# First chunk's values on SyncE's queue with a cast on chip, and a new rank for every step, in a gated linear attention followed by a mixture of experts

## The chip, the cores and the metric

The kernel runs on one core of one Trainium2 chip. The metric is device time in microseconds (us) of one execution. Five engines work side by side: TensorE (PE, matrix multiplication; PEld is its weight load), VectorE (DVE), ScalarE (ACT), GpSimd (POOL) and SyncE (SP, which here only issues transfers). Transfers (DMA) are issued by SP and by POOL, each with a queue of its own; the transfers that POOL issues can convert a type on the way.

## The reference

```
# attention: B, H, S, D = 4, 8, 768, 48; one state of D x D for each b, h
f = 1 / (1 + exp(-f_logit))
for t in range(S):
    state = f[t][:, None] * state + outer(k[t], v[t])
    y[t] = q[t] @ state
x = y, with the heads of one position side by side      # (3072, 384)
# experts: E = 4, 384 -> 1024 -> 384
p = domain_probs / (sum(domain_probs) + 1e-9)
out = sum over e of  p[:, e] * (relu(x @ w1[e]) @ w2[e])
```

## The kernel before, in words

The sequence is cut into C = 6 chunks of T = 128 positions. Within a chunk attention is done with matrices: the logarithms of the gates are summed along the chunk (`cs`, and `cq` for the queries of chunk 0), exponentials of the sums (`exps`, `expq`) scale q and k (`q`, `k`), both are transposed on PE (`tpq`, `tpk`), the scores `at` are evicted under a triangular mask (`ev_at0`, `ev_at1`; two of them in chunk 0 by ACT with a `mask` step on POOL after it), `y` multiplies the scores with the values v in bf16 (tile `vb`), `kv` and `ev_kv` and `sf` carry the state on. In chunk 0 `y` is evicted, transposed on PE (`xt`) and evicted as x (`ev_xt`). Then follow the experts: `h` is x @ w1 for one expert and 128 (or 4 x 128) columns of the hidden layer, `relu` its eviction, `o` one half of h @ w2 for 128 positions, `ev_o` its weighted sum. Chunk 0 and half of chunk 1 are done so; the other chunks use seven products in place of eight for the second layer (`hs`, `relu_s`, sums `s1` to `s4`, products `p`, L521 to L607).

The order of the work is not that of the source. Every step is declared with `Plan.add` (L64): a name, the engines that may do it with a planned duration for each, what it depends on, which buffers it takes and frees, and a priority. `Plan.run` (L92) then goes through planned time and, for each engine that is free, takes the first step in order of priority whose inputs are ready and whose buffers are free. The list that results is written out once, so each engine has a fixed order on the chip; the chip's own semaphores decide when each step starts. In the kernel before the priority is computed from the step's place in the loops, and a list `MOVES` (L15) shifts some of them. `DMA` is one more engine of the plan; its order is that of SP's queue.

The loads of chunk 0 are the part that the change touches. For each batch b of four, f, k and q (192 KB each) are loaded by SP as fp32 (L290, L292, order at L1035). The values v are loaded by POOL straight into `vb` (L284): a casting transfer, fp32 in memory and 96 KB of bf16 on chip. The weights are loaded by POOL as well, cast to bf16 (L303), in eleven pieces w0 to w10: w0 and w1 are the first layer of expert 0 in two halves, w2 and w3 that of expert 1, w4 and w5 the second layer of expert 0, w6 and later whole layers; w10 is the second layer of expert 3. POOL's own order of transfers is `SEQ` (L1036): v0 v1 v2 w0 v3 w1, then the other weights. `GATE` (L1039) makes the issue of v0 wait until k1 has landed, and that of v1 until k2 has. In later chunks v is loaded by SP as fp32 into the tile `v`, and a step `v` casts it (`cast_v`, L392). Further waits: f1.0 (chunk 1) is issued when w6 has landed, f1.1 when w8 has (L297, L299), w10 when k1.0 has (L307). While PE has nothing to do ahead of the first `h`, it runs matmuls on a constant (L1022) as padding.

Of the kernel before, what the change touches and what calls it, by code (L numbers as in the profile page):

```python
# [14 lines left out]
MOVES = (  # L15
# [21 lines left out]
)  # L37


class Op:  # L40


    def __init__(self, name, costs, emit, prio, deps=(), takes=(), frees=(), lag=0.0):
# [3 lines left out]
        if name.split(" ")[-1].startswith("0.") and {"ACT", "DVE"} & set(costs):  # L47
            self.lag += 0.1
# [5 lines left out]
class Plan:  # L54


    LATENCY = 0.2
# [6 lines left out]
    def add(self, *args, **kw):  # L64
        op = Op(*args, **kw)
# [71 lines left out]
def kernel(  # L137
# [97 lines left out]
    ins = {}  # L235
# [835 lines left out]
```

## Time and profile before

| | us |
|---|---|
| median of 3 runs | 287.46 (287.0 to 287.76) |
| span of the profiled execution, first to last instruction | 285.7 |
| first transfer issued by SP (f0) | 0.80 |
| first expert matmul on PE (L489) | 18.18 |
| first matmul with w10 (L504) | 58.63 |
| last eviction on DVE (L607) starts | 282.41 |

The span is that of one profiled execution, from its first to its last instruction; the time of a run contains what lies around the span as well. In a row of the time line the first two numbers are start and duration, then come engine, line and operation, what it writes and reads, and, in brackets, how long the engine was idle just before and what it waited for. In a row of a group (line, engine, operation, count) stand busy time and mean duration in ns, then the idle time ahead of the group and its releasers. A row for a DMA has its size on chip and the time from issue to landing. A matmul's duration is modelled and covers its way through the array, so rows of PE overlap; what one costs is read from one start to the next.

### The profile page before, as it was taken

What the parts mean: (1) busy time and instruction counts of PE and PEld (TensorE: products, weight loads), DVE (VectorE), ACT (ScalarE), POOL (GpSimd) and SP (SyncE); (2) the same over time, 40 slices, a digit from 0 to 9 for tenths busy, and PEclk for the clock granted to TensorE, in tenths of its full rate; (3) what the DMA queues carried; (4) which work ended last, traced back from release to release, by engine and by line L of the source; (5) the groups of instructions that cost most, each with busy time, mean ns of one, the idle gap of its engine ahead of it and who ended that gap; (6) DMA issues with size and microseconds to landing.
All of it is one profiled execution on the core that took longest, in us unless ns stands there. A gap on an engine that the chain in (4) does not pass through costs nothing.

```text
span 285.7 us, 7476 instructions
## 1 busy us (share of the span) xinstructions
PE 277.4 (97%) x3016; PEld 236.7 (83%) x3020; DVE 196.1 (69%) x402; ACT 180.6 (63%) x336; POOL 114.1 (40%) x186
## 2 busy tenths in 40 slices
PE   6889999999999999999999999999999999999995
PEld 4667555657877999999999998999899998999994
DVE  5794144697779896875888848886888730874374
ACT  6768756568657963586668766658638348836710
POOL 5999101528663760866036756343750000000000
PEclk9999999999999999999999999999999999999999
DMA  6999999999977999999879999989675210050003
GB/s 157 214 199 207 208 192 205 178 202 178 183 142 151 160 197 155 210 184 185 178 150 189 164 224 210 144 191 158 74 164 107 57 55 2 19 122 31 2 0 110
DMA packets 153687, 41.85 MB, mean 146 GB/s; under 512 B 144029, under 2 KB 152861, under 8 KB 153653
## 3 DMA queue, kind: packets, MB, share of 16 engines
q1 hardware_dynamic: 142404, 34.66, 65.0%
q0 software_dynamic: 11248, 6.72, 16.3%
q8 instruction: 23, 0.38, 0.6%
q14 instruction: 12, 0.09, 0.1%
HBM read 31.51 MB, written 4.72 MB: 127 GB/s over the span
## 4 chain that ended last, share of the span: by engine, by line
PE 78%; DMA 14%; POOL 5%; SPq 1%; issue 0%; DVE 0%; POOLq 0%
PE ps_m L521 33%; PE ps_m L580 29%; DMA w_sb<-in_moe_w_dram 10%; PE ps_m L504 6%; PE ps_m L489 4%; DMA k<-in_k_dram 4%; POOL w_sb L303 2%; PE ps_m L428 2%; PE ps_m L455 1%; POOL vb L284 1%; PE ps_m L451 1%; PE ps_m L338 1%; PE ps_m L461 1%; POOL AT L432 1%; SPq L290 1%
## 5 line engine op out<-in xcount | busy, mean ns | idle before, releaser
L521 PE MATMUL ps_m<-x,w_sb 128*128 128x256 bf16 x864 | 104.8, 273 | 0.0
L529 ACT ACTIVATE h<-ps_m 128x512 bf16<-128x512 f32 x111 | 66.2, 598 | 46.1 <-PE ps_m L521 38.8
L521 PEld LDWEIGHTS <-w_sb 128*128 128x128 bf16 x864 | 82.9, 98 | 9.4
L580 PEld LDWEIGHTS <-S 128*128 128x128 bf16 x576 | 48.7, 98 | 0.9
L607 DVE TENSOR_TENSOR o<-ps_m,o 128x192 f32<-128x192 f32 x91 | 31.3, 354 | 22.0 <-PE ps_m L580 21.0
L580 PEld LDWEIGHTS <-h 128*128 128x128 bf16 x432 | 36.2, 98 | 0.6
L504 PE MATMUL ps_m<-w_sb,h 128*128 128x384 bf16 x192 | 35.3, 326 | 0.4 <-DMA w_sb<-in_moe_w_dram 0.4
L489 PE MATMUL ps_m<-x,w_sb 128*128 128x128 bf16 (+2 forms) x260 | 34.5, 281 | 0.6 <-DMA w_sb<-in_moe_w_dram 0.4
L411 ACT ACTIVATE yb<-ps_m,pn 128x384 bf16<-128x384 f32 x54 | 28.1, 584 | 7.7 <-PE ps_m L455 6.4
L476 POOL TENSOR_TENSOR Sf<-Sf,egs 48x192 f32<-48x192 f32 x40 | 21.0, 526 | 27.1 <-DVE Sf L468 17.4
L444 DVE TENSOR_TENSOR AT<-ps_m,mask 128x512 bf16<-128x512 f32 x40 | 25.2, 683 | 8.6 <-PE ps_m L428 8.5
L500 ACT ACTIVATE h<-ps_m 128x512 bf16<-128x512 f32 (+1 forms) x42 | 22.5, 536 | 12.8 <-PE ps_m L489 11.8
L489 PEld LDWEIGHTS <-w_sb 128*128 128x128 bf16 x264 | 21.7, 98 | 9.5 <-DMA w_sb<-in_moe_w_dram 0.6
L544 DVE TENSOR_TENSOR S<-h 128x1024 bf16<-128x1024 bf16 x36 | 25.2, 713 | 6.1 <-ACT h L529 5.5
L580 PE MATMUL ps_m<-ts_sb,S 128*128 128x192 bf16 x288 | 29.2, 246 | 0.0
L580 PE MATMUL ps_m<-w_sb,S 128*128 128x192 bf16 x288 | 28.7, 246 | 0.0
L504 PEld LDWEIGHTS <-h 128*128 128x128 bf16 x192 | 18.3, 98 | 12.5 <-DMA w_sb<-in_moe_w_dram 0.9
L388 POOL TENSOR_TENSOR qk<-q,e 128x384 bf16<-128x384 f32 x19 | 22.7, 1205 | 14.5 <-ACT e L371 9.7
L580 PE MATMUL ps_m<-w_sb,h 128*128 128x192 bf16 x288 | 28.0, 246 | 0.0
L527 DVE TENSOR_SCALAR h<-ps_m 128x512 bf16<-128x512 f32 x33 | 22.4, 691 | 8.1 <-PE ps_m L521 7.5
L371 ACT ACTIVATE e<-ps_m 128x384 f32<-128x384 f32 x40 | 23.4, 704 | 5.8 <-PE ps_m L338 5.4
L388 POOL TENSOR_TENSOR qk<-k,e 128x384 bf16<-128x384 f32 x20 | 20.2, 1016 | 16.7 <-PE ps_m L580 7.4
(87 smaller groups left out, 317.5 us busy)
## 6 DMA issues: line engine op xcount, KB each, us to landing
out_dram<-o SPq DMA_DIRECT2D x23, 192.0 KB, 2.3
w_sb<-in_moe_w_dram POOLq DMA_DIRECT2D x5, 768.0 KB, 16.3
k<-in_k_dram SPq DMA_DIRECT2D x10, 384.0 KB, 5.6
q<-in_q_dram SPq DMA_DIRECT2D x10, 384.0 KB, 5.2
v<-in_v_dram SPq DMA_DIRECT2D x10, 384.0 KB, 5.4
f<-in_f_logit_dram SPq DMA_DIRECT2D x9, 384.0 KB, 4.6
w_sb<-in_moe_w_dram POOLq DMA_DIRECT2D x6, 384.0 KB, 8.6
f<-in_f_logit_dram SPq DMA_DIRECT2D x6, 192.0 KB, 3.7
```

What stands on the lines that cost most here:

```text
L371: nc.scalar.activation(out=o, in_=i, func=AF.Exp, scale=1.0 if j else -1.0)
L388: return engines[eng].tensor_tensor(out=tl("qk", c, b)[:, j, :, 0:D].rearrange("t (i r) d -> t i r d", r=2), in0=tl("qk"[j], c, b // 2)[:, ...
L411: nc.scalar.activation(out=ys, in_=y, func=AF.Copy, scale=pe)
L444: nc.vector.tensor_tensor(out=tl("AT", c, b)[:, r].rearrange("s i t -> s (i t)"), in0=tl("A", c, b, r).rearrange("s i t -> s (i t)"), in1= ...
L489: nc.tensor.matmul(out=hp(c, e, fc, n0, n1, nf)[:, f], lhsT=w1_sb[:, e, kk, (fc + f) * 128:(fc + f + 1) * 128], rhs=tl("xT", c)[:, kk, n0: ...
L500: nc.scalar.activation(out=dst, in_=src, func=AF.Relu)
L504: nc.tensor.matmul(out=tl("op", c, e, nt)[:, 0:Din], lhsT=tl("h", c, e, half_of(c, nt * T))[:, fc, nt * T:(nt + 1) * T], rhs=w2_sb[:, e, f ...
L521: nc.tensor.matmul(out=out_[:, f], lhsT=w1_sb[:, e, kk, (fc + f) * 128:(fc + f + 1) * 128], rhs=tl("xs", c, hf, p)[:, el, kk, :], start=(k ...
L529: nc.scalar.activation(out=dst, in_=tl("hp", c, hf, p, el, fc), func=AF.Relu)
L544: return nc.vector.tensor_tensor(out=o, in0=in0, in1=in1, op=op)
L580: nc.tensor.matmul(out=out_, lhsT=lhs[:, f, :], rhs=rhs[:, f, :], start=(first and el == 0 and f == 0), stop=(el == 1 and f == KH - 1), sk ...
L607: nc.vector.tensor_tensor(out=o, in0=src, in1=o, op=ALU.add)
```

## The change

1. The loads v0 to v3 of chunk 0 go to SP's queue, as fp32 into the tile `v`, in the declared order f0 k0 q0 f1 k1 q1 v0 f2 k2 q2 v1 f3 k3 q3 v2 v3. `SEQ` is gone; POOL's queue holds the weights alone at the start.
2. Four cast steps `v 0.b` are added, on POOL, ACT or DVE.
3. `GATE` now makes the issue of w0 wait until v1 has landed; the two old gates are gone.
4. `MOVES` is replaced by `RANKS`: one number for each of the 1483 steps, in the order in which they are declared, which takes the place of the computed priority; a letter behind it pins the step to ACT (A), DVE (D) or POOL (P).
5. Planned durations are changed, and the planned latency between engines goes from 0.2 to 0.12 us. They act on the order alone.

Read against the steps as they are declared, the ranks give SP's queue the order f0 f1 q0 q1 f2 k1 k0 f3 k2 k3 q2 v1 q3 v0 v2 (probabilities) v3. Some other ranks of the start: expq 0.2 41, gate2 0.3 45, ev_at1 0.1 48 (ACT), q 0.2 50P, v 0.1 56A, mask1 0.1 59 (POOL), issue of w0 63, y 0.1 65, v 0.0 66A, v 0.2 71P, y 0.0 73, xt 0.1 77, issue of w1 79, v 0.3 85P, at 0.3 89, xt 0.0 93, first h 95, y 0.2 104, y 0.3 108. Around w10: cs 1.2 278, o 0.2.1.0 281, o 0.3.2.0 (the first use of w10) 284, o 0.1.3.1 294. A rank is a priority, not yet a place: a step with a higher number goes first where that with the lower one isn't ready in the plan.

```
+RANKS = (
+    "0 8 2 1 6 3 40 4 16 25 29 13 20 35 46 53 63 72 79 88 90 101 107 119 117 132 129 145 137 156 177 153 178 159 193 166 230 "
...
-    LATENCY = 0.2
+    LATENCY = 0.12
...
-        self.moves = dict(m.split("=") for m in MOVES.split(";") if m)
+        self.ranks = RANKS.split()
...
-        by, _, engine = self.moves.get(op.name, "0").partition("@")
-        op.prio += float(by)
-        if engine:
+        rank = self.ranks[len(self.ops)]
+        op.prio = int(rank.rstrip("ADP"))
+        if rank[-1] in "ADP":
+            engine = {"A": "ACT", "D": "DVE", "P": "POOL"}[rank[-1]]
             op.costs = {engine: op.costs[engine]}
...
     def load(c, nm, b, n):
-        if (c, nm) == (0, "v"):
-            ins[c, nm, b] = nc.gpsimd.dma_start(out=tl("vb", c, b), in_=srcs[nm][c, :, b * H:(b + n) * H, :])
-            if f"v{b}" in GATE:
-                after(ins[c, nm, b], ins[GATE[f"v{b}"]])
-            return
...
-        op = P.add(f"ld {nm}{c}.{b}", {"DMA": cost or (1.05 if c else 0.8 if nm in PAIRED else 1.1) * n}, lambda e: load(c, nm, b, n), prio,
-                   deps=deps, takes=[(nm, c, b // 2)], lag=2.0)
+        op = P.add(f"ld {nm}{c}.{b}", {"DMA": cost or (0.85 if c else 0.66 if nm in PAIRED else 0.85) * n}, lambda e: load(c, nm, b, n), prio,
+                   deps=deps, takes=[(nm, c, b // 2)], lag=2.0 if c else 2.5)
...
-        if x[0] == "v":
-            issued.append(P.add(f"v issue {i}", {"POOL": 0.8}, lambda _, i=i: load(0, "v", i, 1), -600 + 2 * j,
-                                deps=issued[-1:] + gate(x), takes=[("vb", 0, i)], lag=1.2))
-            ld[0, "v", i] = P.add(f"ld v0.{i}", {"DMA": 1.1}, lambda _: None, VW[0] + j, deps=issued[-1:] + fifo[-1:], lag=2.0)
-            fifo.append(ld[0, "v", i])
-            continue
-        e, which, ks, cols = pieces[i]
+    for j, (e, which, ks, cols) in enumerate(pieces):
+        i, x = j, f"w{j}"
...
-            vb = ld[0, "v", b] if c == 0 else P.add(f"v {c}.{b}", {"POOL": 0.52, "ACT": 0.52} if c == 1 else {"POOL": 0.5}, one(cast_v), s(4),
+            vb = P.add(f"v {c}.{b}", {"POOL": 0.52, "ACT": 0.53, "DVE": 0.45} if c == 0 else {"POOL": 0.52, "ACT": 0.52} if c == 1 else {"POOL": 0.5}, one(cast_v), s(4),
                        deps=[ld[c, "v", b]], takes=[("vb", c, b)], frees=[("v", c, half)])
...
-ORDER = "f0 k0 q0 f1 k1 q1 f2 f3 k2 q2 k3 q3"
-SEQ = "v0 v1 v2 w0 v3 w1"
+ORDER = "f0 k0 q0 f1 k1 q1 v0 f2 k2 q2 v1 f3 k3 q3 v2 v3"
...
-GATE = {"v0": (0, "k", 1), "v1": (0, "k", 2)}
+GATE = {"w0": (0, "v", 1)}
```

More of the change, by code (lines that the diff above doesn't have):

```diff
@@ L717, in attention @@
         for bs in pairs:
-            at = P.add(f"at {c}.{bs[-1]}", {"PE": 0.5 if c == 0 and "q" in PAIRED else 0.43 if len(bs) == 1 else 0.66}, lambda e, bs=bs: [pe_at(c, b) for b in bs], slot(bs[-1], 7),
+            at = P.add(f"at {c}.{bs[-1]}", {"PE": 0.48 if len(bs) == 1 else 0.7}, lambda e, bs=bs: [pe_at(c, b) for b in bs], slot(bs[-1], 7),
                        deps=[t for b in bs for t in ET[b]], takes=[("ps_m", "A", c, b, r) for b in bs for r in range(2)], lag=0.2,
@@ L728, in attention @@
             at, vb = AT_[b], VB[b]
-            eA = [P.add(f"ev_at{r} {c}.{b}", {"ACT": 0.6} if c == 0 and f"{b}.{r}" in BYPOOL.split() else {"DVE": 0.685}, one(ev_at, r), s(7) + 0.1 + 0.1 * r, deps=[at],
+            eA = [P.add(f"ev_at{r} {c}.{b}", {"ACT": 0.735} if c == 0 and f"{b}.{r}" in BYPOOL.split() else {"DVE": 0.685 if c else 0.73}, one(ev_at, r), s(7) + 0.1 + 0.1 * r, deps=[at],
                         takes=[("AT", c, b)], frees=[pt_("A", r)]) for r in range(2)]
@@ L732, in attention @@
                 if c == 0 and f"{b}.{r}" in BYPOOL.split():
-                    eA[r] = P.add(f"mask{r} {c}.{b}", {"POOL": 0.65}, on(mask_at, r), s(7) + 0.2 + 0.1 * r, deps=[eA[r]])
-            y = P.add(f"y {c}.{b}", {"PE": 0.4 if c else 0.28}, on(pe_y), s(11), deps=eA + [vb, kvdone.get((c - 1, b))],
+                    eA[r] = P.add(f"mask{r} {c}.{b}", {"POOL": 0.8}, on(mask_at, r), s(7) + 0.2 + 0.1 * r, deps=[eA[r]])
+            y = P.add(f"y {c}.{b}", {"PE": 0.386 if c else 0.21}, on(pe_y), s(11), deps=eA + [vb, kvdone.get((c - 1, b))],
                       takes=[pt_("y")], frees=[("QK", c, b), ("AT", c, b), ("vb", c, b)], lag=0.2)
@@ L751, in attention @@
             cs_ = lambda ks: slice(ks.start * 128, ks.stop * 128)
-            ey = [P.add(f"ev_y {c}.{b}", {"ACT": 0.48, "DVE": 0.56} if c else {"ACT": 0.4, "DVE": 0.47} if len(parts) == 1 else {"ACT": 0.3, "DVE": 0.36},
+            ey = [P.add(f"ev_y {c}.{b}", {"ACT": 0.48, "DVE": 0.56} if c else {"ACT": 0.49, "DVE": 0.55} if len(parts) == 1 else {"ACT": 0.3, "DVE": 0.42},
                         lambda e, b=b, ks=ks: copy(e, tl("yb", c, b)[:, cs_(ks)], tl("y", c, b)[:, cs_(ks)]), s(11) + 0.1,
@@ L760, in attention @@
                     xdone[c, b].append(
-                        P.add(f"ev_xt {c}.{b}", {"ACT": 0.48, "DVE": 0.4} if c else {"ACT": 0.4, "DVE": 0.3} if len(parts) == 1 else {"ACT": 0.3, "DVE": 0.25},
+                        P.add(f"ev_xt {c}.{b}", {"ACT": 0.48, "DVE": 0.4} if c else {"ACT": 0.47, "DVE": 0.36} if len(parts) == 1 else {"ACT": 0.35, "DVE": 0.25},
                               lambda e, b=b, ks=ks: copy(e, tl("xT", c)[:, ks, b * T:(b + 1) * T], tl("xp", c, b, ks.start)[:, ks]),
```

29 lines of the change are left out of this document (12 added, 17 removed), and 75 rows, old and new, of tables (MOVES, RANKS).

## The prediction

> **What bounds the kernel now.** I read the page first, then busy time by stage, then the waits of TensorE (PE).
>
> ```profile
> PE 277.4 (97%) x3016; PEld 236.7 (83%) x3020; DVE 196.1 (69%) x402; ACT 180.6 (63%) x336; POOL 114.1 (40%) x186
> ```
>
> 97% is an average over stages, and its first part contains matmuls that only keep PE busy (L1022). So I cut the span where PE starts its first real expert matmul (18.18 us), where it first uses the last weights (58.63) and where the last matmul has been drained (282.40):
>
> ```profile
> core 0: us, PE busy (x) PEld busy (x) DVE busy (x) ACT busy (x) POOL busy (x), PEclk, DMA share, GB/s
> 0.00:18.18 18.18, 13.78 (x146) 9.58 (x146) 12.89 (x31) 11.60 (x26) 14.20 (x29) 1.00 1.20 187
> 18.18:58.63 40.45, 39.87 (x327) 24.52 (x332) 19.55 (x40) 27.24 (x46) 15.69 (x28) 1.00 1.19 200
> 58.63:282.40 223.77, 223.74 (x2544) 202.56 (x2544) 163.27 (x332) 141.72 (x265) 84.25 (x130) 1.00 0.73 134
> ```
>
> In the third stage PE has 0.03 us free in 223.77, at a granted clock of 1.00: no new order can gain there, it can only lose. What can be won lies ahead of 18.18 and in one wait at 58.63. The waits of PE say the same (total us, times, longest):
>
> ```profile
> PE ps_m L428 <- DVE QK L279: 1.3, 3, 0.6
> ...
> PE ps_m L489 <- DMA w_sb<-in_moe_w_dram: 0.4, 1, 0.4
> PE ps_m L504 <- DMA w_sb<-in_moe_w_dram: 0.4, 1, 0.4
> ```
>
> The first belongs to the start-up; the other two are for weights. In order of time:
>
> ```profile
> 10.43 0.77 POOL L303 DMA_DIRECT2D w_sb<-in_moe_w_dram  x1
> ...
> 16.21 0.47 ACT L278 COPY x<-ps_m 128x384 bf16<-128x384 bf16 x1
> ...
> 18.18 0.84 PE L489 MATMUL ps_m<-x,w_sb 128*128 128x128 bf16 x12 [0.41 <-DMA w_sb<-in_moe_w_dram]
> ...
> 18.86 0.33 PE L480 MATMUL ps_m<-ident,yb 128*128 128x128 bf16 x3
> ...
> 19.12 0.41 PE L428 MATMUL ps_m<-QK 48*128 48x128 bf16 x8
> ...
> 19.46 0.37 PE L455 MATMUL ps_m<-vb,AT 128*128 128x48 bf16 x8
> ```
>
> The first batch's input x is ready at 16.68 (16.21 + 0.47), but the first expert matmul starts at 18.18, when weight piece w0 has landed. w0 was issued at 10.43, behind three casting loads of v. So the start of the dense stage, call it S, is set by w0, not by attention; the other end of that stage is set by w10:
>
> ```profile
> 48.32 0.94 POOL L303 DMA_DIRECT2D w_sb<-in_moe_w_dram  x1 [18.70 <-DMA k<-in_k_dram]
> ...
> 58.63 0.82 PE L504 MATMUL ps_m<-w_sb,h 128*128 128x384 bf16 x4 [0.37 <-DMA w_sb<-in_moe_w_dram]
> ```
>
> w10 arrives 40.45 us after S, and PE waits 0.37 us for it. Both ends of this stage are DMA.
>
> **The change, part by part.** Removed from POOL: four issues of v. Added: four casts (rank list: batches 0 and 1 on ScalarE, 2 and 3 on POOL).
>
> ```profile
> 7.61 2.84 POOL L284 DMA_DIRECT2D vb<-in_v_dram  x3 [2.66 <-DMA k<-in_k_dram]
> ...
> 11.16 0.94 POOL L284 DMA_DIRECT2D vb<-in_v_dram  x1
> ```
>
> ```profile
> 54.22 0.50 ACT L278 CAST vb<-v 128x384 bf16<-128x384 f32 x1
> ...
> 56.52 0.52 POOL L279 CAST vb<-v 128x384 bf16<-128x384 f32 x1
> ```
>
> POOL gives back 2.84 + 0.94 = 3.78 us and pays 2 x 0.52 = 1.04; ACT pays 2 x 0.50 = 1.00. That is not the path by itself. What matters is the wait that takes the place of the old one: w0 is now issued only after v1 has landed (GATE), and POOL, which runs in order, has a product (q 0.2, pinned to POOL) and a mask (mask1 0.1) ranked ahead of it.
>
> First the gate. v1 is the twelfth load on SP's queue:
>
> ```profile
> 7.59 0.63 SPq L290 DMA_DIRECT2D f<-in_f_logit_dram  x1
> ...
> 11.53 0.52 ACT L325 ACTIVATE f<-f 128x384 f32<-128x384 f32 x1 [0.34 <-DMA f<-in_f_logit_dram]
> ```
>
> The tenth load was issued at 7.59 and landed at 11.53. Two more at 0.63 each put v1 at about 12.8; 11.9 if the issues are never held up. SP then still issues q3, v0, v2, v3 and the probabilities, so the cast of v0 on ACT comes at about 14.5; y 0.0 waits for it, and that is hidden as long as w0 is later.
>
> Then POOL's own queue. q 0.2 needs ACT's chain up to expq 0.2: by ranks eight gate steps, three exps with their small one, three expq, from 3.94:
>
> ```profile
> 3.94 0.52 ACT L325 ACTIVATE f<-f 128x384 f32<-128x384 f32 x1 [1.85 <-DMA f<-in_f_logit_dram]
> ```
>
> ```profile
> L330 ACT ACTIVATE gp<-f 128x384 bf16<-128x384 f32 x4 | 2.1, 520 | 0.1
> L378 ACT ACTIVATE e<-ps_m 128x384 f32<-128x384 f32 x4 | 2.0, 492 | 0.8 <-PE ps_m L353 0.8
> L373 ACT ACTIVATE e<-ps_m 128x384 f32<-128x384 f32 x4 | 2.0, 491 | 0.4 <-PE ps_m L346 0.3
> ...
> L375 ACT ACTIVATE egs<-ps_m 112x4 f32<-112x4 f32 x4 | 0.7, 170 | 0.0
> ```
>
> 8 x 0.52 + 3 x (0.49 + 0.17) + 3 x 0.49 = 7.6, so 11.55; the last gate step (0.52) may come behind expq 0.2, which then ends between 11.0 and 11.6. POOL's part:
>
> ```profile
> L388 POOL TENSOR_TENSOR qk<-q,e 128x384 bf16<-128x384 f32 x19 | 22.7, 1205 | 14.5 <-ACT e L371 9.7
> ```
>
> ```profile
> 14.74 1.30 POOL L432 TENSOR_SCALAR_AFFINE_SELECT AT<-AT 128x512 bf16<-128x512 bf16 x1
> ...
> 18.30 0.66 POOL L432 TENSOR_SCALAR_AFFINE_SELECT AT<-AT 128x512 bf16<-128x512 bf16 x1
> ```
>
> q 0.2 runs 1.2 us, to about 12.8 (13.3 if POOL also takes k 0.2 before it). If w0 goes next, it is issued at 12.8; if the mask comes first (its input, an eviction on ACT, is ready at about 12.8), at 12.8 + 0.66 = 13.5 up to 13.3 + 1.3 = 14.6. I take the middle of 12.8 and 14.6, **13.7**, against 10.43 before.
>
> Now how long w0 takes. The trace has no weight load without company; bounds:
>
> ```profile
> egs<-e POOLq DMA_DIRECT2D x16, 2.0 KB, 3.1
> ```
>
> ```profile
> w_sb<-in_moe_w_dram POOLq DMA_DIRECT2D x1, 384.0 KB, 7.7
> ```
>
> ```profile
> DMA to landing us min/median/max: 7.5/10.3/22.9
> ```
>
> A 2 KB load of this queue takes 3.1 us; w0 took 7.7 in company, w1 7.5. In the stream a piece of 768 KB adds the spacing of two landings:
>
> ```profile
> 18.89 0.76 POOL L303 DMA_DIRECT2D w_sb<-in_moe_w_dram  x1
> ...
> 20.13 0.95 POOL L303 DMA_DIRECT2D w_sb<-in_moe_w_dram  x1
> ```
>
> ```profile
> w_sb<-in_moe_w_dram POOLq DMA_DIRECT2D x1, 768.0 KB, 13.6
> ```
>
> ```profile
> w_sb<-in_moe_w_dram POOLq DMA_DIRECT2D x1, 768.0 KB, 16.3
> ```
>
> (20.13 + 16.3) - (18.89 + 13.6) = 3.94, so 1.97 for w0's 384 KB. On this count the sixteen loads of SP are nearly through when w0 is issued, so I take the lower side, 3.1 + 1.97 = **5.0**, with 4.2 (the issue's own 0.8 overlaps the transfer) and 7.5 as ends: S = 13.7 + 5.0 = 18.7, 0.5 later than before. x, ready at 16.68 before, has two us to spare there; an x later than w0 would act as a late w0 does below. The Trainium skill ("DMA: Bandwidth & Descriptors", section "Anatomy of one DMA — SWDGE (gpsimd) path") gives a fixed 2.0 us plus bytes at 436 GB/s: with the 768 KB read, an estimate of 3.8 us, S = 17.5. The 3.1 us for 2 KB speak against so small a fixed part, so it stays with the fast rival.
>
> What is done before S. At 18.18 the transposes of batch 1 and the scores of batch 3 still lay ahead (18.86 to 19.46: 0.6 us); by the ranks they now come ahead of the first h. If nothing else bound, PE would be 0.5 - 0.6 - 0.37 = 0.5 us ahead of before. But w10 does bind. Before, v3 sat between w0 and w1 in POOL's queue:
>
> ```profile
> 13.15 1.58 POOL L303 DMA_DIRECT2D w_sb<-in_moe_w_dram  x2
> ```
>
> w1 landed at 13.15 + 7.5 = 20.65, w0 at 10.43 + 7.7 = 18.13: 2.52 apart, 0.55 more than 1.97. With v3 gone the stream is 0.55 shorter, and w10, gated by the same chain (w8, f1.1, k1.0), lands 40.45 - 0.55 = 39.9 after S. PE needs it earlier: 40.08 of work before, less the 0.6, less o 0.1.3.1, ranked behind the first use of w10, plus cs 1.2, ranked ahead:
>
> ```profile
> 61.09 1.30 PE ps_m L504 x8
> ...
> 87.23 0.33 PE ps_m L338 x2
> ```
>
> four L504 are 0.65, one L338 is 0.17: 40.08 - 0.6 - 0.65 + 0.17 = 39.0 after S. So PE waits 0.9 us for w10. It goes on at 18.7 + 39.9 = 58.6, as before, with 0.65 - 0.17 = 0.48 more left to do. Sum: 58.6 - 58.63 + 0.48 = **+0.45 us**; in short, change = S - 18.25. The third stage I cost at nothing, since it had 0.03 us of waits under the old order (up to 2 us in a rival). The end stays: the last eviction and one store behind it, as before.
>
> The profiled execution's span is 285.7 and would become 286.15; the median of the runs is 287.46, 1.8 above the span, for what lies around it. I add the change to the median: 287.46 + 0.45 = **287.9**.
>
> **The rivals.** Fast start: POOL issues w0 as soon as q 0.2 is done (12.8) and w0, nearly alone, takes 4.2. Then S = 17.0 and the change is 17.0 - 18.25 = -1.25: 286.2. For: the loads on SP no longer compete with casting loads; against: the mask ranked ahead. It decides below S = 17.4. Late w0: w0, behind the mask (14.2) and sharing the engines with the last v loads, takes 6.5. S = 20.7, change +2.45: 289.9, slower. For: no weight load of the trace took under 7.5; against: those had others of their own queue ahead. It decides from S = 19.1 on, and every later weight follows. New order: in the third stage steps that were covered now wait; twenty waits of 0.1 us are 2 us, 289.5 to 290. For: every rank is new and the planned latency falls from 0.2 to 0.12; against: the old order had none. That the change does nothing (w0 as late as it was, w10 as before) gives 287.5 and lies within the forecast.
>
> **How the numbers follow.** Two runs of this kernel can be told apart from about 0.3%, 0.86 us: 286.6 to 288.3 counts as the same. Forecast (S of 17.4 to 19.1) 0.38; fast start 0.30; late w0 0.18; new order 0.14. So faster 0.30, same 0.38, slower 0.18 + 0.14 = 0.32. Point 287.9. The range takes in the fast start down to 286.0 and the late w0 up to 289.9, which leaves out 0.2.
>
> **What would show it.** In the profile after: w0's issue at 12.8 to 14.6 on POOL and its time to landing near 5 (first step); the first L489 waiting for DMA at about 18.7 (second); PE waiting 0.5 to 1.3 us at the first L504 of the last expert at about 58.6 (third); nearly no PE wait from there to 282 (fourth). I am wrong if the first L489 starts before 17.4 or if the wait for w10 is gone, since the whole sum hangs on w10 following w0.

## The result, and the profile after

The changed kernel takes 297.52 us (median of 4 runs, 297.02 to 301.77) where the kernel before takes 287.43 on the same chip: a ratio of 1.0315, 95% interval 1.025 to 1.038. The ratio is that of the fast runs alone, without the slow one of 301.77, so it is not the quotient of the two medians. The changed kernel is 3.1% slower; 287.9 was forecast, and 289.9 was the upper end of the range. The profiled execution's span is 295.4 us against 285.7: 9.7 us to account for. The trace below has the line numbers of the changed kernel (L517 was L489, L608 was L580, L366 was L338, L353 was L325); in the kernels of the experiments they shift by a few lines more.

First busy time by stage, cut at the same times as in the prediction (PE is the first column of busy time, PEclk, DMA share and GB/s are the last three):

```profile
0.00:18.18 18.18, 14.25 (x152) 10.41 (x152) 12.13 (x30) 13.23 (x30) 8.99 (x25) 1.00 0.93 195
18.18:58.63 40.45, 36.05 (x270) 22.16 (x271) 20.77 (x39) 19.63 (x35) 18.69 (x31) 0.92 1.17 189
58.63:282.40 223.77, 221.38 (x2485) 197.33 (x2484) 176.01 (x345) 129.09 (x244) 83.13 (x130) 1.00 0.72 136
```

The second stage has 4.4 us without PE where it had 0.6, at a granted clock of 0.92 instead of 1.00; the third has 2.4 where it had 0.03. PE's waits in order of time:

```profile
19.59 1.89 PE L517 MATMUL ps_m<-x,w_sb 128*128 128x128 bf16 x24 [1.46 <-DMA w_sb<-in_moe_w_dram]
...
51.50 0.80 PE L366 MATMUL ps_m<-gp,Ub 128*128 128x384 bf16 x2 [2.99 <-ACT gp L361]
...
131.71 0.82 PE L608 MATMUL ps_m<-w_sb,S 128*128 128x192 bf16 x8 [0.96 <-ACT o L311]
...
143.77 1.47 PE L549 MATMUL ps_m<-x,w_sb 128*128 128x256 bf16 x12 [0.73 <-ACT h L557]
...
157.58 0.82 PE L549 MATMUL ps_m<-x,w_sb 128*128 128x256 bf16 x6 [0.70 <-ACT yb L439]
```

The wait for w10 at 58.63 is gone. The first wait is that of the forecast: S is 19.59. The second is new: cs 1.0, the first sum of chunk 1's gates. In the kernel before PE came to it without a wait:

```profile
50.60 0.49 PE L338 MATMUL ps_m<-gp,Ub 128*128 128x384 bf16 x2
```

The releaser now is the second gate step on ACT (gp, L361); the first one (f, L353) had itself waited for a transfer, as had many gate steps after it (time line of ACT, then the waits by releaser: total us, times, longest):

```profile
49.39 0.84 ACT L353 ACTIVATE f<-f 128x768 f32<-128x768 f32 x1 [7.40 <-DMA f<-in_f_logit_dram]
...
125.16 0.84 ACT L353 ACTIVATE f<-f 128x768 f32<-128x768 f32 x1 [3.43 <-DMA f<-in_f_logit_dram]
...
129.41 0.84 ACT L353 ACTIVATE f<-f 128x768 f32<-128x768 f32 x1 [1.56 <-DMA f<-in_f_logit_dram]
```

```profile
ACT f L353 <- DMA f<-in_f_logit_dram: 18.6, 10, 7.4
```

In the kernel before that row reads:

```profile
ACT f L325 <- DMA f<-in_f_logit_dram: 2.2, 2, 1.8
```

ACT works in order, so a gate step that waits for f holds every eviction behind it, and PE waits for those at 131.71, 143.77 and 157.58: the releaser named there is ACT, the cause stands in front of it on ACT.

The third thing the trace shows is the clock. Busy time in steps of 1 us:

```profile
20.00:21.00 1.00, 1.00 (x18) 1.00 (x16) 0.15 (x1) 0.53 (x1) 1.00 (x2) 0.78 1.19 165
21.00:22.00 1.00, 1.00 (x19) 1.00 (x17) 0.16 (x1) 0.56 (x2) 1.00 (x3) 0.50 1.06 147
22.00:23.00 1.00, 1.00 (x19) 1.00 (x17) 0.97 (x3) 0.64 (x3) 0.94 (x3) 0.50 1.31 183
23.00:24.00 1.00, 1.00 (x12) 1.00 (x11) 0.04 (x1) 0.02 (x1) 1.00 (x3) 0.51 0.95 134
...
51.00:52.00 1.00, 0.50 (x2) 0.26 (x2) 0.00 (x0) 0.94 (x2) 0.63 (x1) 0.64 1.14 235
52.00:53.00 1.00, 1.00 (x4) 0.36 (x3) 0.00 (x0) 0.98 (x2) 0.31 (x1) 0.50 1.25 241
53.00:54.00 1.00, 1.00 (x4) 0.40 (x3) 0.38 (x1) 1.00 (x3) 0.66 (x1) 0.50 1.13 143
54.00:55.00 1.00, 1.00 (x5) 0.38 (x3) 1.00 (x2) 0.87 (x2) 0.90 (x2) 0.65 1.10 151
```

After each of the two long waits PE looks busy but runs at half clock for about 3.4 us: (1 - 0.78) + 0.50 + 0.50 + 0.49 = 1.7 us of work lost, and about as much (1.6) the second time. A busy share alone would not show this.

The account of the span's +9.7 us, by these rows: S 19.59 - 18.18 = +1.4; attention already done before S about -0.5 (an estimate from the rows behind S); half clock +1.7; wait at cs 1.0 +3.0; half clock +1.6; the three waits behind ACT +2.4; w10's wait -0.4. That is 9.2; 0.5 is unassigned. It says where time is lost in one execution, not what each term is worth. The two half clocks show that: by their mean clock, the runs of 297.02 and 297.93 us (0.994) had about one such stretch, that of 297.12 (0.988) two (0.006 of 295 us is 1.8 us, what one costs PE), and having one fewer did not make a run clearly faster. What causes the loss, and which terms depend on each other, the experiments had to tell.

### The profile page after: what moved, and what is told of

Read it like the earlier page. It is cut to its first block, busy times and chain, and to the rows that moved or that the text cites. A ratio compares the mean times of both kernels' runs of the same rounds, so it can differ in the third digit from the quotient of the medians.

```text
span 295.4 us, 7488 instructions
## 1 busy us (share of the span) xinstructions
PE 281.1 (95%) x3016; PEld 239.1 (81%) x3016; DVE 215.6 (73%) x431; ACT 162.3 (55%) x308; POOL 110.8 (38%) x185
## 4 chain that ended last, share of the span: by engine, by line
PE 73%; DMA 16%; SPq 5%; ACT 2%; POOL 2%; DVE 1%; issue 1%; ACTq 0%; POOLq 0%; DVEq 0%
PE ps_m L549 27%; PE ps_m L608 25%; PE ps_m L532 8%; DMA w_sb<-in_moe_w_dram 7%; DMA f<-in_f_logit_dram 6%; PE ps_m L517 6%; SPq L320 2%; PE ps_m L456 2%; SPq L318 2%; PE ps_m L483 1%; DMA q<-in_q_dram 1%; DMA x<-yb 1%; PE ps_m L366 1%; PE ps_m L479 1%; PE ps_m L489 1%
## 5 line engine op out<-in xcount | busy, mean ns | idle before, releaser
L549 PEld LDWEIGHTS <-w_sb 128*128 128x128 bf16 x864 | 82.7, 98 | 11.0 <-issue 1.8
L557 ACT ACTIVATE h<-ps_m 128x512 bf16<-128x512 f32 x100 | 59.2, 597 | 51.0 <-PE ps_m L549 43.7
L608 PEld LDWEIGHTS <-S 128*128 128x128 bf16 x576 | 48.4, 98 | 2.2 <-issue 1.1
L555 DVE TENSOR_SCALAR h<-ps_m 128x512 bf16<-128x512 f32 x44 | 30.1, 686 | 15.1 <-PE ps_m L549 14.3
L517 PE MATMUL ps_m<-x,w_sb 128*128 128x128 bf16 (+2 forms) x264 | 36.5, 295 | 1.5 <-DMA w_sb<-in_moe_w_dram 1.5
L608 PEld LDWEIGHTS <-h 128*128 128x128 bf16 x432 | 36.4, 98 | 0.9
L517 PEld LDWEIGHTS <-w_sb 128*128 128x128 bf16 x264 | 23.0, 103 | 11.6 <-DMA w_sb<-in_moe_w_dram 2.0
L526 DVE TENSOR_SCALAR h<-ps_m 128x256 bf16<-128x256 f32 (+1 forms) x29 | 15.3, 549 | 21.2 <-PE ps_m L517 18.8
L572 DVE TENSOR_TENSOR S<-h 128x1024 bf16<-128x1024 bf16 x36 | 28.2, 793 | 2.7 <-ACT h L557 2.0
L608 PE MATMUL ps_m<-w_sb,S 128*128 128x192 bf16 x288 | 28.3, 246 | 1.0 <-ACT o L311 1.0
L608 PE MATMUL ps_m<-ts_sb,S 128*128 128x192 bf16 x288 | 28.8, 246 | 0.0
L608 PE MATMUL ps_m<-w_sb,h 128*128 128x192 bf16 x288 | 28.2, 246 | 0.0
L416 POOL TENSOR_TENSOR qk<-k,e 128x384 bf16<-128x384 f32 x21 | 21.4, 1020 | 15.8 <-ACT egs L403 5.8
L439 ACT ACTIVATE yb<-ps_m,pn 128x384 bf16<-128x384 f32 x42 | 22.6, 579 | 5.7 <-DVE yb L441 3.5
L312 POOL CAST vb<-v 128x384 bf16<-128x384 f32 x18 | 9.0, 501 | 43.5 <-PE ps_m L489 31.8
```

The lines of the kernel that those rows point to most:

```text
L416: return engines[eng].tensor_tensor(out=tl("qk", c, b)[:, j, :, 0:D].rearrange("t (i r) d -> t i r d", r=2), in0=tl("qk"[j], c, b // 2)[:, ...
L439: nc.scalar.activation(out=ys, in_=y, func=AF.Copy, scale=pe)
L517: nc.tensor.matmul(out=hp(c, e, fc, n0, n1, nf)[:, f], lhsT=w1_sb[:, e, kk, (fc + f) * 128:(fc + f + 1) * 128], rhs=tl("xT", c)[:, kk, n0: ...
L549: nc.tensor.matmul(out=out_[:, f], lhsT=w1_sb[:, e, kk, (fc + f) * 128:(fc + f + 1) * 128], rhs=tl("xs", c, hf, p)[:, el, kk, :], start=(k ...
L555: nc.vector.tensor_relu(out=dst, in_=tl("hp", c, hf, p, el, fc))
L557: nc.scalar.activation(out=dst, in_=tl("hp", c, hf, p, el, fc), func=AF.Relu)
```

## The experiments

Two theories at the start. **Order**: the new order asks for transfers at times at which they can't have arrived, at three places (w0; f1.1; the later loads of f). **Values**: fp32 values on SP's queue delay the whole stream of transfers. A third, **clock**: the clock falls by itself. Kernels that ran side by side on one chip are compared with each other, others by their ratio to the kernel before; runs of one changed kernel spread by 1 to 4 us, so differences under 0.5% between two of them settle nothing.

### Values or order?

The kernel before, its order kept, with v loaded by SP as fp32 (v0 and v1 ahead of q2, q3 and k3 in SP's queue), and casts:

```
-        if (c, nm) == (0, "v"):
-            ins[c, nm, b] = nc.gpsimd.dma_start(out=tl("vb", c, b), in_=srcs[nm][c, :, b * H:(b + n) * H, :])
...
+        if i == 0:
+            after(ins["w", i], ins[0, "v", 1])
...
+    for b, e in enumerate(("ACT", "ACT", "POOL", "POOL")):
+        o = Op(f"v 0.{b}", {e: 0.5}, lambda g, b=b: cast_v(0, b, g), 0)
```

> The kernel before, its order of steps as it was, with the first part of the change alone: v of chunk 0 loaded by SP as fp32, two casts on ACT and two on POOL, w0 issued when v1 has landed. Theory A (the time is lost by the new order of steps, which waits at three places for transfers, and by the clock that is halved after two of them): the first expert matmul starts between 17.5 and 19.0 us, there is no wait of PE over 1 us behind it, and the time is 287.0 to 288.5. Theory B (the values as fp32 on SP delay the whole stream of transfers, and all later waits follow from that): 290 or more, with PE waiting for chunk 1's f or for a weight between 45 and 60 us.

Measured 293.78 us, 1.0203 (1.0139 to 1.0267): slower than theory "order" had it. The number is that of "values", but the wait which that theory named (for chunk 1's f or a weight, at 45 to 60 us) is not there. The loads of v delayed what attention needed:

```profile
20.73 0.61 PE L394 MATMUL ps_m<-ident,qk 128*128 128x128 bf16 x4 [1.75 <-DVE qk L382]
```

PE waits for a product of q at 20.73, and the first expert matmul starts at 22.2; from 16 to 26 us PE runs at half clock. Then the reverse: the new order and its casting loads on POOL as before, no casts, w0 behind v0 and v1:

```
+        if (c, nm) == (0, "v"):
+            ins[c, nm, b] = nc.gpsimd.dma_start(out=tl("vb", c, b), in_=srcs[nm][c, :, b * H:(b + n) * H, :])
...
+    done = [o for o in done if not (o.name.startswith("v 0.") or o.name.startswith("ld v0."))]
```

> The changed kernel's order of steps, with v of chunk 0 loaded by POOL's casting queue as before (v1, v0, w0 ahead of POOL's first product, v2 and v3 where their casts stood, no cast steps). Theory A: the wait for w0 goes, so about 1.5 us and the 1.7 us of the halved clock behind it, but the wait of cs 1.0 for chunk 1's gates (3 us), the halved clock behind that (1.5 us) and the waits of 130 to 158 us (2.4 us) stay: 293 to 295. Theory B: most of the 10 us is gone, 287 to 290.

Measured 297.36, 1.0324 (1.0288 to 1.0359): as large a loss, without any of the value part. The wait for w0 is gone, but the wait at cs 1.0 and the one behind the held gate steps are there as in the changed kernel. The first of these rows is a wait that the changed kernel does not have, for a product that POOL now does behind the loads of v and w0:

```profile
15.45 0.61 PE L428 MATMUL ps_m<-ident,qk 128*128 128x128 bf16 x4 [1.87 <-POOL qk L416]
...
52.30 0.80 PE L369 MATMUL ps_m<-gp,Ub 128*128 128x384 bf16 x2 [2.41 <-ACT gp L364]
...
133.06 0.82 PE L611 MATMUL ps_m<-w_sb,S 128*128 128x192 bf16 x8 [1.03 <-ACT o L311]
```

So **the new order is enough for a loss of this size**, and under it the value path makes no difference that these runs can tell (1.0324 and 1.0315). Two limits: the issues were put into POOL's order by hand, and the wait at 15.45 comes with that, so the start of this kernel is not that of the changed one; and its first expert matmul comes late as well, at 20.65. The half clock is not needed for the loss: one of the four runs had a mean clock of 1.0 and took 296.75 us, the others 296.71 to 298.11.

### What makes cs 1.0 wait

Padding matmuls ahead of the first expert matmul, to keep the clock up, and an earlier issue of f1.1:

```
+    next(o for o in done if o.name.startswith("h 0.")).pad = 7
```

> The changed kernel with seven matmuls on a constant ahead of the first expert matmul on PE, which fill the 1.6 us in which PE waits for w0. Theory A: w0 lands as before, the granted clock stays at 1.00 from 20 to 24 us instead of 0.50, and the time falls by 1.5 to 1.8 us, to about 295.8. Rival C (the clock falls for another reason than the idle time, as power): it falls all the same, 297.5.

```
+        if (c, nm, b) == (1, "k", 0):
+            after(ins[c, nm, b], ins["w", w_gate])
...
-            after(ins[c, nm, b], ins["w", w_gate])
+            after(ins[c, nm, b], ins["w", 6])
```

> The changed kernel, with the load f1.1 (chunk 1) issued when w6 has landed and not when w8 has; k1.0 now waits for w8 itself. Theory A: chunk 1's gates are done before PE comes to cs 1.0, its wait of 3.0 us and the halved clock behind it (1.5 us) go, less up to 1 us by which w7 and w8 land later: 293 to 294. Theory B (the transfers as a whole are late, and PE would wait for the next weight instead): 296.5 to 297.5, with a wait for w8 or w9 of 3 us.

Measured 298.98 (1.0384) and 298.84 (1.0379): neither gained anything. With padding the clock stayed at 1.00 from 20 to 25 us, but PE then waited longer at cs 1.0: 3.2 us, against 2.1 in the other and 2.3 in the changed kernel on this chip (below). With f1.1 issued early, SP's two loads of f go out together at 35.55, 7 us sooner than f1.1 did; yet it landed only at 50.66 (SP, then ACT):

```profile
35.55 0.99 SPq L320 DMA_DIRECT2D f<-in_f_logit_dram  x2
```

```profile
50.66 0.84 ACT L355 ACTIVATE f<-f 128x768 f32<-128x768 f32 x1 [6.47 <-DMA f<-in_f_logit_dram]
```

14 us from issue to landing. Theory "order" had to be made sharper (**stream**): f1.1 lands when what lies ahead of it is through, and whatever PE wins before cs 1.0 it waits for there. The page of the changed kernel has the busy share of the sixteen DMA engines in 40 slices of 7.4 us, in tenths:

```profile
DMA  6999999998999989999999979434265070700002
```

From 7 us on they are busy throughout for the first 60 us and beyond. Busy is not the same as fast: from 16 to 26 us they moved 162 GB/s in this kernel, 201 in the kernel before. The next kernels, with the changed kernel beside them on one chip, tested "stream".

> The changed kernel itself, so that the next three have it beside them on one chip. Both theories: ratio 1.03 to 1.04 to the kernel before. The start-up differs from chip to chip: the first expert matmul at 19.6 in the first trace, at about 21.1 in the trace with the early f load.

Measured 300.07, 1.0334 (1.0251 to 1.0416), beside 290.82 for the kernel before on this chip. cs 1.0 moved about 3.5 us later in the order:

```
+    for x in ("cs 1.0", "cs 1.1", "exps 1.0", "exps 1.1"):
+        put(x, "h 0.3.5.0")
+    for x, ahead in (("gate1 1.0", "relu 0.3.0.0"), ("gate1 1.2", "gate2 1.2"), ("q 1.0", "t 2.1")):
+        put(x, ahead)
...
+    for x in ("tpk 1.0", "tpq 1.0", "ev_tp 1.0"):
+        put(x, "o 0.2.3.0")
```

> The changed kernel with the gates of f1.0 and f1.1, their two sums (cs 1.0, cs 1.1) and what follows from them moved about 3.5 us later in the order of TensorE, ScalarE, VectorE and GpSimd; the transfers are as they were. Theory 'order': the order asks for f1.1 5 us before the stream of transfers can bring it; moved later, the wait of 3.0 us falls below 1 us and the half clock behind it (1.5 us) goes: 3 to 4 us faster than the changed kernel on this chip. Rival 'stream': the transfers are the bound whatever the order, and the wait comes back at the next step that needs one (w10 or k1): within 1 us of the changed kernel.

Measured 297.74, 1.0258 (1.0178 to 1.0337): 2.3 us less than the changed kernel, not 3 to 4. The wait at cs 1.0 and the half clock at 51 to 55 us are gone (1.00 there), so the clock doesn't fall by itself at that place; a wait of half its size has come up behind it (and see the two kernels with cs 1.0 later on another chip, further down):

```profile
55.73 0.81 PE L517 MATMUL ps_m<-x,w_sb 128*128 128x512 bf16 x3 [1.52 <-ACT e L399]
```

w0 ahead of POOL's products and mask, gated on k0.0 in place of v1:

```
-            after(ins["w", i], ins[GATE[f"w{i}"]])
+            after(ins["w", i], ins[0, "k", 0])
...
+    put("w issue 0", "k 0.2")
```

> The changed kernel with w0 issued on GpSimd ahead of the two products instead of behind products and mask, as soon as k0.0 has landed instead of v1. Theory 'order': the first expert matmul starts at about 18 instead of 19.6 to 21, without the half clock behind it: 2 to 3.5 us faster than the changed kernel. Rival 'stream': the sixteen DMA engines are full from 1 to 50 us, f1.1 lands when it did, and what is won at the start is waited for at cs 1.0: within 0.7 us of the changed kernel.

Measured 300.17, 1.0337: no change. The number is that of "stream", but its mechanism was not tested, since nothing was won at the start. w0 is issued at 9.36 instead of 14.6, but the loads that attention needs come later for it: PE waits 1.5 us for a product at 16.95, and the first expert matmul starts at 22. The weights behind w0 don't come earlier either (w1 is issued at 19.42). And cs 1.0 waits as before:

```profile
16.95 0.61 PE L425 MATMUL ps_m<-ident,qk 128*128 128x128 bf16 x4 [1.53 <-POOL qk L413]
...
54.20 0.48 PE L366 MATMUL ps_m<-gp,Ub 128*128 128x384 bf16 x2 [3.09 <-ACT gp L361]
```

Then bytes were taken out of the stream. Half of w7 and of w8 is not loaded; zeros stand in their place, so half of two experts' layers is missing from the output:

```
+        if i == 7:
+            ks = slice(0, KF // 2)
+        if i == 8:
+            cols = slice(0, F // 2)
```

> The changed kernel with half of the weight pieces w7 and w8 not loaded (zeros in their place, set by GpSimd while it is idle at 5 to 10 us): 2 x 384 KB on chip less in the stream ahead of f1.1. The order is as it was. Theory 'stream': f1.1 lands about 4 us earlier (2 x 1.97), the wait of 2.3 to 3.2 us at cs 1.0 and the half clock behind it are gone: 4 us faster than the changed kernel, a ratio of 1.017 to 1.022. Rival 'queue or landing latency': f1.1 is late because of its own issue and landing time, not of what is ahead of it: cs 1.0 still waits over 1.5 us, 1.028 or more.

Measured 293.34, 1.0207 (1.0144 to 1.027). f1.1 lands 3 us earlier than in the changed kernel (49.99 on the other chip), and cs 1.0 no longer waits:

```profile
47.01 0.84 ACT L359 ACTIVATE f<-f 128x768 f32<-128x768 f32 x1 [3.26 <-DMA f<-in_f_logit_dram]
```

```profile
50.10 0.49 PE L372 MATMUL ps_m<-gp,Ub 128*128 128x384 bf16 x2
```

So f1.1's landing follows the bytes ahead of it: an earlier issue (14 us on the way) doesn't bring it, fewer bytes do. In time, the interval still overlaps a little with that of the changed kernel, which ran on other chips (1.025 to 1.038).

### The later loads of f

Five loads of f two to four transfers earlier in SP's queue:

```
+    put("ld f3.2", "ld v3.0")
+    put("ld f4.0", "ld v3.0")
+    put("ld f4.2", "ld q4.0")
+    put("ld f5.2", "xs 2.3.0")
+    put("ld f5.0", "ld q4.2")
```

> The changed kernel with five later loads of f (f3.2, f4.0, f4.2, f5.0, f5.2) issued two to four transfers earlier on SyncE's queue. Theory 'order': gate steps on ScalarE no longer wait for f from 120 to 160 us, evictions behind them aren't held, and the waits of PE behind those (2.4 us) go: 2 to 2.5 us faster than the changed kernel. Rival: those waits come from something else, or move to the loads that now come later (q, v): within 0.7 us of the changed kernel.

Measured 303.07, 1.0454: 3.0 us slower than the changed kernel, against both expectations. The waits behind ACT are gone; in their place PE waits for the transposes of x behind f5.2 on SP's queue. These start 0.8 us later than in the changed kernel on this chip (134.61, there 133.81), and PE comes to the step that needs them 3.5 us sooner (136.3, there 139.83); the remaining 1.3 us were not followed up:

```profile
141.93 5.63 PE L549 MATMUL ps_m<-x,w_sb 128*128 128x256 bf16 x30 [5.63 <-DMA x<-yb]
```

With cs 1.0 later and only f3.2 and f4.0 moved:

> The kernel with cs 1.0 later, and f3.2 and f4.0 issued ahead of v3.0 on SyncE's queue (the other three loads of f stay where they are). Theory 'order': the long waits of ScalarE for f at 125 and 129 us go, with the wait of 1.0 us of PE behind them; 0.5 to 1.5 us faster than with cs 1.0 later alone (1.0258): 1.020 to 1.024. Rival: what is issued earlier delays the transposes behind it, as in the kernel with five loads moved: 1.026 or more.

Measured 297.78, 1.032 (1.0257 to 1.0382): nothing gained, not even the 2.3 us that cs 1.0 later had brought; PE still has 9.22, 9.06 and 9.01 us of each ten from 130 to 160. Then one number of the planner instead of steps moved by hand:

```
-                   deps=deps, takes=[(nm, c, b // 2)], lag=2.0 if c else 2.5)
+                   deps=deps, takes=[(nm, c, b // 2)], lag=4.0 if c else 2.5)
```

> The changed kernel with one number of its planner changed: a load of the later chunks counts as landed 4.0 us after its turn on the DMA engines instead of 2.0 (a piece of 384 KB is then planned at 5.7 us from issue to landing; the trace has 5 to 5.5). All ranks and edits stay; the planner puts other steps first while it waits (cs 1.0 at 47.1 instead of 45.2 in the plan). Theory 'order made for too early landings': the held gates on ScalarE and half of the wait at cs 1.0 go, 2 to 4 us faster than the changed kernel, a ratio of 1.018 to 1.027 to the kernel before. Rival: the ranks themselves are at fault wherever transfers land: 1.03 or more.

The profiled execution has a span of 293.6, but the four runs spread from 295.31 to 299.56 us: median 298.14, 1.0347 (1.0277 to 1.0416). By the median the rival is right. The trace shows the trade:

```profile
60.00:80.00 20.00, 18.42 (x173) 13.53 (x171) 14.34 (x32) 11.80 (x24) 10.80 (x18) 1.00 1.10 208
80.00:100.00 20.00, 19.32 (x189) 13.75 (x187) 17.15 (x33) 12.83 (x25) 13.32 (x20) 1.00 1.05 194
120.00:130.00 10.00, 10.00 (x140) 9.40 (x139) 8.92 (x19) 6.33 (x10) 1.58 (x4) 1.00 1.10 202
130.00:140.00 10.00, 10.00 (x105) 9.19 (x103) 8.78 (x20) 8.33 (x15) 6.55 (x12) 1.00 1.09 182
```

From 120 to 160 PE is full again, and cs 1.0 waits 0.4 us instead of 3.0; from 60 to 100 it now has 2.3 us of waits that the changed kernel does not have.

### Does the sum close?

The planner's later landing together with the half pieces (same part left out):

> The changed kernel with the planner's later landing (4.0) and half of w7 and w8 left out (zeros in their place). Theory 'sum': waits at cs 1.0 gone (f1.1 lands at about 47), held gates on ScalarE gone; what is left is the late start (1.4 to 2.7 us), a half clock behind it (1.6) and about 2 us of other waits of the planner's new order: 1.012 to 1.020. Rival: the two cures don't add, 1.0207 as with half pieces alone or more.

Measured 295.08, 1.0239 (1.0203 to 1.0275): above the expected 1.012 to 1.020. The cures don't add up. The profiled span is 291.9, 6.2 above the kernel before. What its trace still has is the start, and 2.0 us of small waits between 80 and 180:

```profile
20.07 1.51 PE L523 MATMUL ps_m<-x,w_sb 128*128 128x128 bf16 x24 [0.35 <-DMA w_sb<-in_moe_w_dram]
23.71 0.84 PE L523 MATMUL ps_m<-x,w_sb 128*128 128x128 bf16 x12 [1.36 <-DMA w_sb<-in_moe_w_dram]
```

S + 1.9 and 1.4 for w1 make 3.3. Two kernels went after the start: four padding matmuls, and v2 and v3 not loaded (zeros in their place, so those two batches of chunk 0 are missing as well).

> As the kernel with late landing and half pieces, with four matmuls that only keep PE busy ahead of the first expert matmul. Theory 'clock by idleness': no half clock at 20 to 25 us, and as no later wait swallows the gain, 1 to 1.6 us faster than without the padding (0.004 to 0.0055 of the ratio). Rival: the clock falls for another reason or the weights swallow it: within 0.5 us of it.

> As the kernel with late landing and half pieces, with the loads of v2 and v3 of the first chunk left out as well (zeros in their place). Theory 'stream': w0 shares the sixteen engines with what SyncE has issued before it; two loads of 192 KB less ahead of it bring the first expert matmul 1.5 to 2 us earlier (at 18 to 19) and the end with it: 0.005 to 0.007 less in the ratio. Rival 'issue': w0's landing follows from its own issue on GpSimd at 13.7 to 14.7 and 5 to 6 us of its own: the first expert matmul moves by under 0.5 us.

Measured 294.43, 1.0221 (1.0156 to 1.0286), and 293.83, 1.0207 (1.0176 to 1.0237). The first says nothing of the clock: the profile without padding had no half clock at all, the one with it had 0.75 from 20 to 25 us. The same holds for padding with cs 1.0 later:

> The kernel with cs 1.0 later, and seven matmuls that only keep PE busy ahead of the first expert matmul. With the wait at cs 1.0 still there such padding gained nothing (1.0384 beside 1.0379). Theory 'stream': what is won at the start was waited for at cs 1.0; with that wait gone, the half clock at 20 to 25 us costs its 1.5 us, and without it this kernel is 1 to 1.5 us faster than with cs 1.0 later alone: 1.020 to 1.023. Rival: the half clock at the start costs nothing because the weights bound that stage: 1.0245 or more.

Measured 296.83, 1.0312 (1.028 to 1.0343): no gain. So two kernels with cs 1.0 later (1.032 and 1.0312) lie no lower than the changed kernel itself (1.0315 and 1.0334), and the 2.3 us rest on the runs of one chip. Here the padding itself was caught by a half clock (an idle stretch of 1.17 us ended at 17.80), took 3.0 us instead of 1.3 and pushed the first expert matmul to 22.62:

```profile
17.80 0.64 PE L343 MATMUL ps_m<-ident,o 24*128 24x24 f32 x4 [1.17 <-DMA o<-in_moe_domain_probs_dram]
...
19.64 3.19 PE L1061 MATMUL ps_m<-S 128*128 128x512 bf16 x7
22.62 1.59 PE L517 MATMUL ps_m<-x,w_sb 128*128 128x128 bf16 x13
```

The kernel without v2 and v3 has w0 issued at 14.71 and landed at 19.80: 5.1 us instead of 5.9 (14.20 to 20.07). So the two loads cost w0 0.8 us, but its issue slid by 0.5, of which 0.4 is the fill with zeros that stands in POOL's queue just ahead; S moved 0.3, and would have moved 0.7 without the fill (an estimate). By its number "issue" (under 0.5) is right and "stream" (1.5 to 2) is not; but with the fill in the way the 0.8 us speak for a share of both. **What makes the start late stays open** between w0's issue behind POOL's products and the shared engines.

### Is the value part free in some other place?

Three more kernels with the old order: v0 behind f3, v1 behind q3, v2 and v3 ahead of the probabilities, w0 once q1 has landed; then v0 behind q2, v1 behind f3, the probabilities ahead of v2 and v3; then the same with w0 gated on v0:

```
-            after(ins["w", i], ins[0, "v", 1])
+            after(ins["w", i], ins[0, "q", 1])
...
+        after_ = ("ld q0.2", "ld f0.3", "ld p", "v issue 2")[b]
+        done.insert(1 + next(i for i, y in enumerate(done) if y.name == after_), x)
```

> The kernel before with its own order, its four values loaded as fp32 by SyncE's queue and cast on ScalarE (0, 1) and GpSimd (2, 3), but each load of v put behind the loads of f and q that the first batches need (v0 behind f3, v1 behind q3, v2 and v3 last), and w0 issued as soon as q1 has landed. With v ahead of q2, q3 and k3 the old order gave 1.0203, its first expert matmul at 22.2. Theory 'place': loading v on SyncE's queue costs nothing by itself; the first expert matmul comes at 18 to 19 and the time is 0.998 to 1.006 of the kernel before. Rival 'bytes': fp32 values put 0.39 MB more into a full stream, 2 us at 195 GB/s, ahead of w10: 1.008 or more even so.

> The kernel with its old order and values by SyncE's queue again (v0 behind q2, v1 behind f3), but with the small load of the probabilities ahead of v2 and v3, not behind them; behind them it landed only at 29.7 us, and PE stood still for 9.9 us before. w0 is issued once q1 has landed. Theory 'place': without that wait the first expert matmul comes at 18 to 20 and the time is 1.000 to 1.010 of the kernel before: loading v as fp32 costs little by itself. Rival 'bytes': the fp32 values and their casts cost 2% in any place, as in the first run with the old order: 1.015 or more.

> As the kernel with the probabilities first, but w0 is issued only once v0 has landed. Theory 'place': w0 then takes no share from v0 and k3, but comes 1 to 2 us later itself: within 0.5% of the other, first expert matmul at 19 to 21. Rival 'w0 is late by its issue': S follows w0's issue, and the time is 1 to 2 us more than with the earlier gate.

Measured 300.31, 1.0444 (1.0403 to 1.0484); 298.80, 1.0411 (1.0353 to 1.0469); 294.33, 1.0194 (1.0129 to 1.0258). "Place" as I had it fell three times. In the first, PE stood still for a load of 48 KB that was issued at 17.16, behind the weights in the shared engines:

```profile
29.75 0.64 PE L312 MATMUL ps_m<-ident,o 24*128 24x24 f32 x4 [9.92 <-DMA o<-in_moe_domain_probs_dram]
```

In the second v2 and v3, issued from 13.35 to 16.8, come that late, and POOL's casts wait for them ahead of weight issues:

```profile
24.83 0.50 POOL L279 CAST vb<-v 128x384 bf16<-128x384 f32 x1 [4.96 <-DMA v<-in_v_dram]
...
30.39 0.50 POOL L279 CAST vb<-v 128x384 bf16<-128x384 f32 x1 [2.56 <-DMA v<-in_v_dram]
```

w0's later gate takes 4.5 us off that, which neither expectation had (no change, or 1 to 2 us dearer); why was not found. In the best two of four places under the old order the value part costs 2%; whether a better place makes it free was not found. No kernel here beats the kernel before.

## Why the prediction was wrong

- **w0's issue on POOL**: forecast 13.7 (12.8 to 14.6), measured 13.75 behind product and mask. So close a hit is in part luck: 13.7 was the middle of a range, and the product did not start when ACT's chain was done (11.6 in the forecast) but at 12.21, when its q had landed:

```profile
12.21 1.00 POOL L413 TENSOR_TENSOR qk<-q,e 128x384 bf16<-128x384 f32 x1 [0.49 <-DMA q<-in_q_dram]
13.17 0.63 POOL L460 TENSOR_SCALAR_AFFINE_SELECT AT<-AT 128x512 bf16<-128x512 bf16 x1
13.75 0.92 POOL L331 DMA_DIRECT2D w_sb<-in_moe_w_dram  x1
```

- **w0's landing**: forecast 5.0 later, measured 5.8; S 19.59 instead of 18.7. This is the late w0 rival (S from 19.1 on), whose formula S - 18.25 gives +1.3. The term was mis-sized by 0.8 us: the stream was not nearly through when w0 went out, and in the kernel with two loads fewer w0's time fell by just that much (5.9 to 5.1). The Trainium skill ("DMA: Bandwidth & Descriptors", section "Anatomy of one DMA — SWDGE (gpsimd) path") would give 3.8 for it, the estimate that the prediction made from that page; the measured 5.8 decides.
- **Work done before S**: forecast 0.6, measured about 0.5.
- **"w10 does bind", PE waits 0.9 for it**: this step failed. w10's wait is gone, and the prediction had named just that as a sign of being wrong. With S as measured its sum gives +1.3 us; the other 8.4 of the span's 9.7 lie where it had nothing. It followed w10 through its chain (w8, f1.1, k1.0) but never asked when the new order itself needs f1.1. The planner of each kernel says it; in its own planned time:

```
before: ld f1.1 46.70 to 47.75, gate1 1.0 49.95, cs 1.0 52.17
after:  ld f1.1 39.19 to 40.04, gate1 1.0 42.16, cs 1.0 45.17
```

  In the plan the order asks for f1.1 (by gate1 1.0) 7.8 us earlier; in PE's own order cs 1.0 stands about 5 us of work earlier (32.4 us behind S before, 28.9 now, 1.7 of them by the half clock). The chip does not bring f1.1 earlier. SP had issued it, the second of these two, by 43.98, and it landed at 49.39; the kernel before started that gate step at 47.40:

```profile
35.00 8.98 SPq L320 DMA_DIRECT2D f<-in_f_logit_dram  x2
```

```profile
47.40 0.83 ACT L325 ACTIVATE f<-f 128x768 f32<-128x768 f32 x1
```

  The change itself shows where the plan's optimism comes from. The larger part is one pair of ranks: 207 for f1.1 and 230 for the transfer of w9. The planner of before has w9 ahead of f1.1 (42.30 to 46.70), the new one behind it (45.14 to 49.19); with w9 put ahead again, the new planner has gate1 1.0 at 46.21, 4.05 us later. But the plan's transfer of a weight emits nothing on the chip, where w9 goes out with POOL's issue at 30.55, 13 us ahead of f1.1's. The rest is cheaper transfers: the planned cost of 192 KB goes from 1.05 to 0.85, of a whole weight layer from 4.4 to 4.05. The profile of before has 200 GB/s in this stage: 384 KB are 1.97 us by that (an estimate), not 2 x 0.85 = 1.7; and a load of f from issue to landing is planned at 1.7 + 2.0 + 0.12 = 3.8, where the list of transfers after has

```profile
f<-in_f_logit_dram SPq DMA_DIRECT2D x9, 384.0 KB, 5.4
```

  There is a second side, which no experiment took apart: f1.1 also goes out 3 us later (issued by 43.98, before by 41.02), since w8, whose landing it waits for, comes later. POOL issues w1 to w9 from 16.04 to 30.55 us, before from 13.15 to 22.64, and it is from 16 to 26 that the rate falls to 162 GB/s. Under the new order only w0 was ever moved forward, so how much of the wait at cs 1.0 is early demand and how much late supply stays open.

- **"The third stage I cost at nothing"**: failed too; 2.4 us, the size of the new-order rival (2 us, chance 0.14), but by three waits behind held gate steps on ACT, not by twenty of 0.1.
- **The half clock** (1.7 and 1.6 us in the trace) was in no step and no rival.
- **The end**: right. The last eviction starts 3.6 us ahead of the span's end (291.82), before 3.3.

What is shown: the new order is enough for a loss of this size; f1.1's landing follows the bytes ahead of it; moving the demand later or the bytes away removes the wait at cs 1.0 (2.3 us of the 9.7 on one chip, no gain in the two kernels on another that contain the same move; 1.0207 in place of 1.0315 to 1.0334 with the bytes gone). What is only argued: that w9's place and too short transfers in the plan are why the ranks are as they are. What stays open: the late start, the later issues of the weights, the price of the value loads, and why a cure at one place so often comes back as a wait at another; the account above is of one execution, and its terms are not independent.

## What to carry to other kernels

Where a plan fixes the order of an in-order machine, read its planned costs in the diff like code, and ask whether the chip will keep the plan's order of transfers: an order that counts a weight as coming later, while its issue goes out first, asks for data before they can be there. For each transfer that the new order needs earlier, ask what is ahead of it in the stream; here, with the DMA engines busy, an earlier issue of that one load brought nothing. And a third stage without slack under the old order is a reason to price a new order above nothing, since every wait there is a full loss.

## What the runs showed of the hardware

**Half clock behind short waits.** After 1.46 us without work PE ran at half clock for 3.4 us, after 2.99 again; in the kernel with the planner's later landing a wait of 0.81 us ahead of 14.08 was enough (clock 0.50 from 15 to 18 us). But the length of one wait does not decide: in the kernel before waits of 0.58 and 0.41 us had no such effect, and neither had 1.53 us ahead of 16.95 in the kernel with w0 early (clock 1.00 from 17 to 26) or 1.36 us ahead of 23.71 in the one with half pieces and later landing. With matmuls in place of the wait the clock stayed at 1.00 in one kernel, but not in two others. Nor is 3.4 us the only length: worked out from the clock in steps of 1 us, the stretch lasted 6.8 us with cs 1.0 later (18.7 to 25.5) and 10.2 in the second profile of the changed kernel (14.8 to 25.0), two and three times 3.4, though PE was busy for 9.5 of the 10 us from 15 to 25. The Trainium skill ("TensorE: Matmul & The Clock Gate", section "Part 1: The HAM clock gate (the "warmup" mystery)") has the clock fall after an idle window of about 3.4 us and rise after as long a busy one. The shortest stretch here agrees with that length; the waits that set it off were shorter, and the long stretches went on while PE was busy. The price where nothing swallows it: on one chip the kernel before ran at a mean clock of 0.986 to 0.987 in four of six runs, 290.81 to 291.51 us, and once at 0.998: 287.81.

**A small load can take 12 us.** 48 KB of probabilities were issued at 17.16 and let PE go on at 29.75; in the changed kernel the same load, issued at 12.68, had landed when PE came to it at 16.10. f1.1 took 14 us once. In these traces the time from issue to landing followed what was ahead of a transfer, not how large it was.
